# Gated linear attention feeding a softplus-erf expert layer on one core: most signs of the float64 weights written by ScalarE, and another fixed order of all steps

## The chip, the core and the metric

The kernel runs on one NeuronCore of a Trainium2 chip. The core has a matrix engine (TensorE, PE in the profile), a vector engine (VectorE, DVE), a scalar engine (ScalarE, ACT), GpSimd (POOL) and SyncE (SP), which here only issues DMAs. Matmuls accumulate in PSUM; the engines' other operands lie in SBUF. The metric is the device time of one execution, in microseconds (us). In this program a float32 product on PE appears as two records of the trace, and a product in the rounded format fp32r (`F32R`) as one.

## The reference, cut to what matters

```
def _attn_ref(q, k, v, alpha):                # each (4, 8, 768, 48)
    state = zeros((B, H, D, D)); y = zeros_like(q)
    for t in range(S):
        state = alpha[:, :, t, :, None] * state + einsum('bhd,bhe->bhde', k[:, :, t], v[:, :, t])
        y[:, :, t] = einsum('bhd,bhde->bhe', q[:, :, t], state)
    return y
def _moe_ref(x, w_in, w_out):                 # x (3072, 384), w_in (384, 2048), w_out (2048, 384)
    h = x @ w_in
    sp = np.maximum(h, 0.0) + np.log1p(np.exp(-np.abs(h)))
    return ((h * erf(sp)) @ w_out).astype(np.float32)
def reference(...):                           # x: the attention output, heads side by side
    x = attn_out.transpose(0, 2, 1, 3).reshape(B * S, H * D)
    return _moe_ref(x=x, **moe_kwargs)
```

`w_in` and `w_out` arrive as float64, everything else as float32.

## The kernel before, in words

**Order.** The whole program is a list of 1664 steps in the string `ORDER` (L31). The loop at its end runs through the list and calls the function of each step, and each of the four queues PE, DVE, ACT and SP executes its instructions exactly in that order: `Queue.call` (L211) chains every instruction to the one before it on its engine, which is why nearly all rows of the profile carry L211. Nothing is reordered at run time. An engine that waits holds up all its later instructions.

**Attention.** Time is cut into 12 parts of 64 steps, and the batch into two halves: 24 chunks n. Chunk n loads alpha, k, q, v (`la lk lq lv`); DVE runs two scans (`sb`, `sa`), takes a reciprocal (`rc`), scales k and q (`kk`, `qq`), masks the scores (`mk`) and updates the state (`td`, and `ta`, which is ACT's in the first two chunks). PE transposes k (`pn`) and makes the scores (`ps`), the outputs (`qt`, `sv`, into the single PSUM tile `py`) and the state's increment (`pu`); `pn`, `ps` and `pu` share one PSUM tile, `both`. ACT copies the transposed k (`kn`; `kd` does it on DVE), a small check value (`ic`), and rounds the result to `x_hi` (`xh`). The rest `x_lo` is made either by DVE as a difference (`xl`) or by PE, which adds minus·x_hi into `py` (`xp`, two products of 128x192), and by ACT, which copies it out (`xe`).

**Expert layer.** A block n of 256 tokens takes its x from chunks 2n and 2n+1. The 2048 hidden columns are 4 groups g of 512, each in two halves. `hm_n_g_half` is 18 products of 128x256 (hi·hi, lo·hi, hi·lo), into one of two PSUM buffers `h__111`, `h__112`; `he` (ACT) or `hd` (DVE) copies it out; `u n1 n2 n3 g` on ACT and `ma mb z1 z2` on DVE work out the activation on 128x1024, with ACT's tables changed between the two sets; `ga` (ACT) or `gd` (DVE) rounds the result to `gh`, `gl` (DVE) keeps the rest; `om_n_g_half` adds 12 products of 128x384 into `acc`. `oe` (ACT) or `ob` (DVE) scales the sums out, `od` stores them. All 24 chunks and 12 blocks are interleaved in `ORDER`.

**Weights.** They stay in SBUF as pairs hi, lo of fp32r. There are 12 tiles of `w_in` (128x512, steps `w?i_n`; group g uses tiles 3g to 3g+2) and 16 of `w_out` (128x384, `w?o_n`). A float64 number arrives as two 32-bit words, so a tile is 512 or 384 KB. The steps on one tile: `wl` loads it; `wy` (ACT) scales the high word into y; `wc` (ACT, from one byte) or `wv` (DVE, by a shift) makes the three low bits z; `wa` (DVE) makes z = (y << 3) | z, and `wb` (DVE, a second such pass) puts in the sign of y. `wh` (ACT) or `wk` (DVE) rounds z to hi; lo is made by DVE as a difference (`wq`), or by PE, z − hi into a PSUM buffer (`wp`, the same two buffers that `hm` uses), and a copy of ACT (`we`). Two more steps are in both files, unused before: `wd` (ACT) writes the high word, scaled, as a 16-bit float into the upper half of z, and so leaves its sign there; `wf` (ACT) writes the low bits as a 16-bit integer into the lower half. Together they stand in place of `wc` and `wb`.

**Dummy products.** `dw_n` issues n float32 products of the 128x128 identity, which nothing reads.

Of the kernel before, what the change touches and what calls it, by code (L numbers as in the profile page):

```python
# [36 lines left out]
wyo_2 xh_1 wbi_1 whi_1 wei_6 wpi_8 ta_0 la_2 sb_2 wao_2 wlo_12 wyo_12 dw_1 wpi_1 pn_1 wei_8 wbi_5 whi_5 wpi_5
wli_11 wco_12 kn_1 wbo_2 wei_1 wli_9 who_2 rc_2 ic_2 xl_1 wei_5 sa_2 hm_0_0_0 wao_12 td_2 lq_2 wyi_11 wbo_12
wlo_0 lk_2 wco_0 wqo_2 lv_2 wli_10 who_12 hm_0_0_1 kk_2 pu_1 qq_2 ps_2 wqo_12 wyo_0 wao_0 wci_9 wci_11 wai_11
he_0_0_0 la_3 sb_3 wbi_11 wbo_0 wci_10 wyi_10 he_0_0_1 wai_10 wyi_9 wai_9 lk_3 hm_0_1_0 mk_2 qt_2 u_0_0 rc_3  # L40
hm_0_2_0 sv_2 lq_3 ta_1 wbi_9 sa_3 wlo_1 wbi_10 he_0_1_0 whi_11 whi_9 who_0 td_3 wqi_11 la_4 qq_3 wvo_1 kk_3
wqo_0 he_0_2_0 whi_10 wyo_1 wao_1 sb_4 wqi_9 n1_0_0 xh_2 xl_2 pn_2 kn_2 n2_0_0 wqi_10 ic_3 hm_0_1_1 he_0_1_1
n3_0_0 hm_0_2_1 he_0_2_1 wbo_1 rc_4 who_1 pu_2 ps_3 wlo_3 wyo_3 lq_4 lk_4 wlo_7 mk_3 ta_2 qt_3 ma_0_0 g_0_0 sa_4
wlo_6 mb_0_0 wqo_1 hm_0_3_0 z1_0_0 wco_3 wao_3 lv_3 sv_3 xh_3 xl_3 kk_4 pn_3 he_0_3_0 wyo_7 hm_0_3_1 kn_3 ic_4
z2_0_0 td_4 lk_5 he_0_3_1 la_5 wco_7 wco_6 hm_1_0_0 qq_4 wlo_9 wyo_6 sb_5 u_0_1 wao_7 wbo_3 ga_0_0_0 gl_0_0_0
hm_1_1_0 he_1_0_0 ga_0_0_1 gl_0_0_1 wao_6 u_0_2 n1_0_1 pu_3 ps_4 n1_0_2 rc_5 n2_0_1 qt_4 om_0_0_0 hm_1_0_1 wbo_7
who_7 mk_4 ta_3 lv_4 sv_4 sa_5 td_5 who_3 wqo_3 kk_5 n3_0_1 he_1_1_0 ma_0_1 wbo_6 pn_4 wqo_7 mb_0_1 he_1_0_1
n2_0_2 kn_4 lq_5 qq_5 n3_0_2 who_6 ma_0_2 la_6 xh_4 xl_4 om_0_0_1 wyo_9 wco_9 wao_9 wqo_6 mb_0_2 g_0_1 z1_0_1
wlo_11 wyo_11 hm_1_2_0 he_1_2_0 wbo_9 lk_6 z2_0_1 lv_5 hm_1_3_0 he_1_3_0 g_0_2 z1_0_2 pu_4 wco_11 ps_5 mk_5 lq_6
wlo_8 wco_8 wyo_8 wlo_4 z2_0_2 qt_5 wao_8 ga_0_1_1 wlo_5 hm_1_3_1 he_1_3_1 hm_1_2_1 wco_4 wlo_13 wyo_4 wao_11  # L50
u_0_3 gl_0_1_1 hm_1_1_1 wlo_10 u_1_0 wbo_8 ta_4 ga_0_2_0 om_0_1_1 wbo_11 sv_5 ic_5 who_9 wqo_9 who_8 n1_0_3
gl_0_2_0 wqo_8 om_0_2_0 sb_6 he_1_1_1 lv_6 wao_4 td_6 ga_0_1_0 gl_0_1_0 pn_5 wbo_4 xh_5 he_1_2_1 rc_6 xl_5
hm_2_1_0 hm_2_1_1 wyo_5 who_11 wqo_11 wco_5 wko_4 sa_6 wao_5 qq_6 qt_6 kn_5 pu_5 wyo_10 wlo_14 wco_10 wbo_5
wao_10 kk_6 ps_6 n2_0_3 ga_0_2_1 n1_1_0 who_5 wqo_5 he_2_1_0 wqo_4 om_0_1_0 n3_0_3 gl_0_2_1 wbo_10 ma_0_3
he_2_1_1 wvo_13 hm_2_0_0 mb_0_3 n2_1_0 wyo_13 n3_1_0 wao_13 mk_6 ta_5 wbo_13 who_10 wqo_10 g_0_3 z1_0_3 he_2_0_0
hm_2_0_1 who_13 wqo_13 z2_0_3 wco_14 ma_1_0 pn_6 he_2_0_1 wyo_14 wlo_15 wco_15 wyo_15 wao_14 om_0_2_1 kn_6 sv_6
ga_0_3_0 gl_0_3_0 pu_6 wao_15 ga_0_3_1 gl_0_3_1 xh_6 wbo_14 lv_7 om_0_3_0 u_1_1 lk_7 wbo_15 g_1_0 mb_1_0
hm_2_2_0 ic_6 la_7 who_15 wqo_15 who_14 wqo_14 om_0_3_1 u_1_2 n1_1_2 oe_0_1 od_0_1 oe_0_0 hm_2_2_1 z1_1_0 z2_1_0
ga_1_0_0 sb_7 lq_7 rc_7 gl_1_0_0 gd_1_0_1 n1_1_1 lq_8 xl_6 sa_7 gl_1_0_1 om_1_0_0 n2_1_2 n2_1_1 om_1_0_1
he_2_2_0 qq_7 kk_7 hm_2_3_0 n3_1_1 td_7 ma_1_1 mb_1_1 n3_1_2 he_2_2_1 ps_7 mk_7 qt_7 hm_2_3_1 g_1_1 u_1_3 z1_1_1  # L60
z2_1_1 u_2_1 ic_7 ga_1_1_0 sv_7 xh_7 ta_6 la_8 ga_1_1_1 lv_8 ma_1_2 pn_7 gl_1_1_0 om_1_1_0 gl_1_1_1 om_1_1_1
# [885 lines left out]
```

## Time and profile before

| | |
|---|---|
| time, median of 3 runs | 516.24 us (515.7 to 516.78) |
| span of the profiled execution, first to last instruction | 513.9 us |
| PE busy | 504.0 us (98%) |
| DVE busy | 488.2 us (95%) |
| ACT busy | 465.8 us (91%) |
| POOL busy | 6.5 us (1%) |
| DMA moved | 43.69 MB, mean 85 GB/s |

The profiled execution's own time isn't listed apart from its span; the median of the runs is 2.3 us above that span. Shares are means over the whole span: the first 29 us, in which the first weights and the first two chunks are made ready, look unlike the rest, so the profile has to be read by stretches of time. Instructions on one engine overlap a little: the next one begins some 0.1 us before the former is shown to end, so what an instruction costs its engine is the distance from its start to the next one's start (its pitch) and not its own duration.

### The profile page before, as it was taken

What the parts mean: (1) busy time and instruction counts of PE and PEld (TensorE: products, weight loads), DVE (VectorE), ACT (ScalarE), POOL (GpSimd) and SP (SyncE); (2) the same over time, 40 slices, a digit from 0 to 9 for tenths busy, and PEclk for the clock granted to TensorE, in tenths of its full rate; (3) what the DMA queues carried; (4) which work ended last, traced back from release to release, by engine and by line L of the source; (5) the groups of instructions that cost most, each with busy time, mean ns of one, the idle gap of its engine ahead of it and who ended that gap; (6) DMA issues with size and microseconds to landing.
All of it is one profiled execution on the core that took longest, in us unless ns stands there. A gap on an engine that the chain in (4) does not pass through costs nothing.

```text
span 513.9 us, 16869 instructions
## 1 busy us (share of the span) xinstructions
PE 504.0 (98%) x7465; PEld 481.7 (94%) x7465; DVE 488.2 (95%) x655; ACT 465.8 (91%) x637; POOL 6.5 (1%) x41
## 2 busy tenths in 40 slices
...
GB/s 324 401 200 176 117 188 131 97 81 60 58 74 44 22 99 78 45 73 83 23 78 107 80 41 60 85 15 44 68 111 54 90 58 32 3 1 32 0 32 34
DMA packets 21387, 43.69 MB, mean 85 GB/s; under 512 B 2368, under 2 KB 5440, under 8 KB 21312
## 3 DMA queue, kind: packets, MB, share of 16 engines
...
q8 instruction: 59, 0.97, 0.8%
...
HBM read 37.86 MB, written 4.72 MB: 83 GB/s over the span
## 4 chain that ended last, share of the span: by engine, by line
PE 64%; DVE 18%; ACT 12%; issue 4%; DMA 1%; POOL 1%; DVEq 0%; POOLq 0%; ACTq 0%
PE acc L211 29%; PE h__112 L211 13%; PE h__111 L211 12%; PE both L211 4%; PE py L211 4%; DVE t L211 2%; DVE gl__104 L211 1%; ACT L211 1%; DVE gl__103 L211 1%; DVE w__98 L211 1%; DVE w__100 L211 1%; PE warm L211 1%; ACT w__97 L211 1%; DMA s__87<-in_moe_w_out_dram 1%; DVE w__97 L211 1%
## 5 line engine op out<-in xcount | busy, mean ns | idle before, releaser
L211 ACT ACT_TABLE_LOAD x64 | 82.1, 1283 | 1.9 <-PEq L901 0.9
L211 PE MATMUL acc<-wo_hi,gh__102 128*128 128x384 f32 x192 | 44.7, 346 | 0.1
L211 PE MATMUL acc<-wo_hi,gh__101 128*128 128x384 f32 x192 | 43.9, 348 | 0.1
L211 PE MATMUL acc<-wo_lo,gh__102 128*128 128x384 f32 x192 | 43.0, 337 | 0.2 <-DVE wo_lo L211 0.2
L211 PE MATMUL acc<-wo_hi,gl__104 128*128 128x384 f32 x192 | 43.1, 337 | 0.0
L211 PE MATMUL acc<-wo_lo,gh__101 128*128 128x384 f32 x192 | 41.6, 336 | 0.0
L211 PE MATMUL acc<-wo_hi,gl__103 128*128 128x384 f32 x192 | 41.6, 337 | 0.0
L211 PEld LDWEIGHTS acc<-wo_lo,gh__102 128*128 128x128 f32 x192 | 34.2, 188 | 0.5 <-DVE wo_lo L211 0.5
L211 PEld LDWEIGHTS acc<-wo_hi,gl__104 128*128 128x128 f32 x192 | 34.3, 188 | 0.0
L211 PEld LDWEIGHTS acc<-wo_hi,gl__103 128*128 128x128 f32 x192 | 34.0, 188 | 0.2 <-DVE gl__103 L211 0.2
L211 PEld LDWEIGHTS acc<-wo_lo,gh__101 128*128 128x128 f32 x192 | 34.1, 188 | 0.0
L211 PEld LDWEIGHTS acc<-wo_hi,gh__101 128*128 128x128 f32 x192 | 31.6, 188 | 1.9 <-DVE gh__101 L211 0.4
L211 PEld LDWEIGHTS acc<-wo_hi,gh__102 128*128 128x128 f32 x192 | 32.6, 188 | 0.8 <-DVE gh__102 L211 0.2
L211 DVE TENSOR_TENSOR_SCAN B<-raw_a,back 128x520 f32<-128x520 f32 x24 | 29.6, 1233 | 4.0 <-POOL T L266 3.9
L211 DVE TENSOR_TENSOR_SCAN A<-raw_a,start 128x520 f32<-128x520 f32 x24 | 29.6, 1233 | 0.2
L211 ACT ACTIVATE s__88<-s__88 128x1024 f32<-128x1024 f32 x22 | 23.2, 1056 | 1.0 <-DVE t L211 0.9
L211 ACT ACTIVATE s__86<-s__86 128x1024 f32<-128x1024 f32 x20 | 21.2, 1058 | 1.9 <-DVE t L211 1.8
L211 PE MATMUL h__112<-x_hi__107,wi_hi 128*128 128x256 f32 x144 | 21.7, 286 | 0.3 <-ACT wi_lo L211 0.3
L211 PE MATMUL h__111<-x_hi__107,wi_hi 128*128 128x256 f32 x144 | 21.4, 284 | 0.0
L211 PE MATMUL h__111<-x_hi__108,wi_hi 128*128 128x256 f32 x144 | 21.1, 282 | 0.0
L211 PE MATMUL h__112<-x_hi__108,wi_hi 128*128 128x256 f32 x144 | 21.1, 282 | 0.0
L211 PE MATMUL h__112<-x_lo__109,wi_hi 128*128 128x256 f32 x144 | 21.0, 281 | 0.0
...
## 6 DMA issues: line engine op xcount, KB each, us to landing
...
raw_k<-in_k_dram SPq DMA_DIRECT2D x24, 256.0 KB, 3.1
raw_q<-in_q_dram SPq DMA_DIRECT2D x24, 256.0 KB, 3.3
raw_v__113<-in_v_dram SPq DMA_DIRECT2D x12, 256.0 KB, 3.3
raw_v__114<-in_v_dram SPq DMA_DIRECT2D x12, 256.0 KB, 3.6
out_dram<-o__106 SPq DMA_DIRECT2D x12, 192.0 KB, 2.0
...
```

Source lines behind the costliest of these rows:

```text
L211: ins = made(*args, **kw)
```

## The change: another list of steps

No step's code is altered but one line of `hm`, which now asks whether the block's buffer exists instead of whether the half is 0, since the new list may begin with half 1. All else is the list, 1668 steps long. Counted in the two lists:

| steps | engine | before | after |
|---|---|---|---|
| `wb` sign as a second pass | DVE | 28 | 11 |
| `wc` low bits | ACT | 25 | 3 |
| `wv` low bits | DVE | 3 | 8 |
| `wd`, `wf` 16-bit halves | ACT | 0, 0 | 17, 17 (6 of `w_in`, 11 of `w_out`) |
| `wh` / `wk` rounding to hi | ACT / DVE | 27 / 1 | 11 / 17 |
| `xl` / `xp`+`xe` | DVE / PE+ACT | 24 / 0 | 19 / 5 (chunks 1, 2, 3, 4, 6) |
| `ga` / `gd` | ACT / DVE | 51 / 45 | 44 / 52 |
| `kn` / `kd` (22 that do work) | ACT / DVE | 20 / 2 | 17 / 5 |
| `oe` / `ob` | ACT / DVE | 18 / 6 | 12 / 12 |
| `dw` blocks (products) | PE | 4 (25) | 3 (24) |
| tiles with `wp` before `hm_0_0_0` | PE | 9 | 7 |
| runs of attention products between `hm` and `om` after `hm_0_0_0` | PE | 53 | 42 |

The core of the diff (the rest of the list differs in the same manner):

```
@@ ORDER, its beginning
-la_0 wli_2 wyi_2 wci_2 wli_3 wyi_3 wci_3 sb_0 rc_0 sa_0 wai_2 wbi_2 whi_2 wli_0 wyi_0 wci_0 wai_3 wbi_3 dw_14
+la_0 wli_2 wli_0 wyi_2 lk_0 sb_0 rc_0 sa_0 wci_2 wli_3 dw_14 ic_0 wyi_0 wfi_0 wai_2 wdi_0 kk_0 pn_0 wbi_2 wfi_3 lq_0
...
@@ ORDER, its end
-ma_11_3 ga_11_2_1 f3 mb_11_3 gl_11_2_1 g_11_3 z1_11_3 od_10_0 om_11_2_1 ga_11_2_0 gl_11_2_0 om_11_2_0 z2_11_3
-gd_11_3_1 gl_11_3_1 om_11_3_1 ga_11_3_0 gl_11_3_0 om_11_3_0 oe_11_0 od_11_0 oe_11_1 od_11_1
+od_10_1 ga_11_2_0 om_11_1_0 ma_11_3 g_11_3 od_10_0 gl_11_2_0 mb_11_3 ga_11_2_1 z1_11_3 gl_11_2_1 om_11_2_0 z2_11_3
+gd_11_3_1 om_11_2_1 gd_11_3_0 gl_11_3_1 gl_11_3_0 om_11_3_1 om_11_3_0 oe_11_1 f2 od_11_1 ob_11_0 f3 od_11_0
...
@@ hm
-            if half == 0:
+            if self.hs[g] is None:
                 self.hs[g] = self.pl.h.tile([P, GT * TB], F32, name="hs", tag="hs")
```

DVE's queue after its first two scans, before (`w__97` to `w__100` are the four buffers in which a weight tile is put together; a `SCALAR_TENSOR_TENSOR` with the name of a buffer on both sides is `wa` or `wb`, "x2" is both):

```order
L211 SCALAR_TENSOR_TENSOR w__97<-w__97 128x512 x2
L211 SCALAR_TENSOR_TENSOR w__98<-w__98 128x512 x2
L211 TENSOR_TENSOR raw_k_118<-raw_k_118,B 128x512
L211 SCALAR_TENSOR_TENSOR w__99<-w__99 128x512 x2
L211 TENSOR_TENSOR raw_q_116<-raw_q_116,A 128x512
L211 SCALAR_TENSOR_TENSOR w__100<-w__100 128x512
L211 SCALAR_TENSOR_TENSOR B<-raw_a,back 128x520
L211 TENSOR_TENSOR sT<-both,mask 128x512
L211 SCALAR_TENSOR_TENSOR w__100<-w__100 128x512
L211 SCALAR_TENSOR_TENSOR w__97<-w__97 128x512
L211 RECIPROCAL start<-B 128x8
```

The same place of DVE's queue after the change:

```order
L205 SCALAR_TENSOR_TENSOR w__97<-w__97 128x512
L205 TENSOR_TENSOR raw_k_118<-raw_k_118,B 128x512
L205 SCALAR_TENSOR_TENSOR w__97<-w__97 128x512
L205 SCALAR_TENSOR_TENSOR w__98<-w__98 128x512
L205 CAST wi_hi<-w__97 128x512
L205 CAST wi_hi<-w__98 128x512
L205 TENSOR_TENSOR raw_q_116<-raw_q_116,A 128x512
L205 TENSOR_SCALAR w__100<-hs__93 128x512
L205 SCALAR_TENSOR_TENSOR w__99<-w__99 128x512
L205 SCALAR_TENSOR_TENSOR B<-raw_a,back 128x520
L205 TENSOR_TENSOR sT<-both,mask 128x512
```

The pairs of passes have become single ones for tile 0 (`w__98`) and tile 3 (`w__99`), and the roundings to `wi_hi` (`CAST`, step `wk`) and one `wv` (`TENSOR_SCALAR`) have come in between.

PE's queue up to the first two thirds of `hm_0_0_0`, before (`h__…<-w__…,ident` and the row below it are one `wp`; `warm` is a dummy product, `both<-ident,raw_k` is `pn_1`):

```order
L211 MATMUL py<-sT,raw_v__114 32x64 x32
L211 MATMUL h__111<-w__99,ident 128x512
L211 MATMUL h__111<-wi_hi,minus 128x512
L211 MATMUL warm<-ident 128x128
L211 MATMUL h__112<-w__97,ident 128x512
L211 MATMUL h__112<-wi_hi,minus 128x512
L211 MATMUL both<-ident,raw_k_119 128x128 x4
L211 MATMUL h__111<-w__100,ident 128x512
L211 MATMUL h__111<-wi_hi,minus 128x512
L211 MATMUL h__112<-x_hi__107,wi_hi 128x256 x6
L211 MATMUL h__112<-x_hi__107,wi_lo 128x256 x6
```

The same place after the change:

```order
L205 MATMUL both<-ident,raw_k_119 128x128 x4
L205 MATMUL warm<-ident 128x128 x3
L205 MATMUL py<-sT,raw_v__114 32x64 x32
L205 MATMUL h__112<-w__99,ident 128x512
L205 MATMUL h__112<-wi_hi,minus 128x512
L205 MATMUL h__111<-w__98,ident 128x512
L205 MATMUL h__111<-wi_hi,minus 128x512
L205 MATMUL py<-x_hi__107,minus 128x192 x2
L205 MATMUL h__112<-x_hi__107,wi_hi 128x256 x6
L205 MATMUL h__112<-x_hi__107,wi_lo 128x256 x6
```

The block of one dummy product is gone, the two `wp` of tiles 8 and 5 no longer stand ahead of `hm_0_0_0`, and `xp_1` (`py<-x_hi__107,minus`) does.

ACT's queue, before, from the rounding of the second chunk's `x_hi` to the copy `wei_1` (its tenth row), which frees the PSUM buffer of `hm_0_0_0`:

```order
L211 ACTIVATE x_hi__107,sums<-py 128x2x3x64
L211 ACTIVATE wi_hi<-w__97 128x512
L211 ACTIVATE wi_lo<-h__112 128x512
L211 ACTIVATE T<-both 128x8x48
L211 ACTIVATE w__99<-s__86 128x384
L211 ACTIVATE wi_lo<-h__111 128x512
L211 ACTIVATE wi_hi<-w__100 128x512
L211 ACTIVATE w__99<-s__86 128x384
L211 ACTIVATE kn<-both 128x384
L211 ACTIVATE wi_lo<-h__112 128x512
L211 ACTIVATE wo_hi<-w__98 128x384
```

After the change, from the rounding of the second chunk's `x_hi` to the `wh` of tile 8:

```order
L205 ACTIVATE x_hi__107,sums<-py 128x2x3x64
L205 ACTIVATE wi_lo<-h__112 128x512
L205 ACTIVATE w__97<-hs__91 128x512
L205 ACTIVATE wi_lo<-h__111 128x512
L205 ACTIVATE x_lo__109<-py 128x2x3x64
L205 ACTIVATE w__97<-hs__91 128x512
L205 ACTIVATE inv<-start 128x8
L205 ACTIVATE wi_hi<-w__100 128x512
L205 ACTIVATE kn<-both 128x384
```

ACT's roundings `wi_hi` have left this place, `xe_1` (`x_lo__109<-py`) has come in, and the instructions on `w_out`'s tiles (128x384) come later.

## Rows read from the trace of the kernel before

**Rows 1.** First line of the profile's page.

```profile
span 513.9 us, 16869 instructions
```

**Rows 2.** Stretches from:to, then length, engines' busy time, granted clock, DMA share, GB/s.

```profile
10.00:29.00 19.00, 17.91 (x282) 11.06 (x281) 18.57 (x31) 18.57 (x41) 0.00 (x0) 1.00 1.03 400
29.00:514.00 485.00, 480.02 (x7154) 464.54 (x7154) 463.74 (x617) 441.21 (x588) 2.17 (x22) 1.00 0.22 68
```

**Rows 3.** Waits of PE's weight loads, 28 to 509 us: total, times, longest.

```profile
PEld h__112 L211 <- ACT wi_lo L211: 0.9, 1, 0.9
PEld acc L211 <- DVE wo_lo L211: 0.5, 1, 0.5
```

**Rows 4.** Timeline of PE, 0 to 34 us: start, duration, operation, idle before.

```profile
11.31 1.02 PE L211 MATMUL h__112<-w__98,ident 128*128 128x512 f32 x2
11.77 0.80 PE L211 MATMUL h__112<-wi_hi,minus 128*128 128x512 f32 x1
12.41 0.83 PE L211 MATMUL warm<-ident 128*128 128x128 f32 x6
...
28.88 0.99 PE L211 MATMUL h__112<-x_hi__107,wi_hi 128*128 128x256 f32 x6 [0.26 <-ACT wi_lo L211]
```

**Rows 5.** Timeline of ACT, 3 to 31 us.

```profile
5.04 1.22 ACT L211 ACTIVATE w__97<-hs__90 128x512 f32<-128x512 f32 x2 [2.56 <-DMA hs__90<-in_moe_w_in_dram]
...
13.33 1.23 ACT L211 ACTIVATE w__97<-hs__94 128x512 int32<-128x512 uint8 x2
14.45 1.25 ACT L211 ACTIVATE w__98<-hs__95 128x512 int32<-128x512 uint8 x2
...
27.36 0.59 ACT L211 ACTIVATE w__99<-s__86 128x384 int32<-128x384 uint8 x1
27.81 0.52 ACT L211 ACTIVATE kn<-both 128x384 f32<-128x384 f32 x1
28.18 0.64 ACT L211 ACTIVATE wi_lo<-h__112 128x512 fp32r<-128x512 f32 x1
```

**Rows 6.** Timeline of DVE, 3 to 31 us.

```profile
3.92 1.24 DVE L211 TENSOR_TENSOR_SCAN B<-raw_a,back 128x520 f32<-128x520 f32 x1 [3.92 <-POOL T L266]
...
20.68 0.55 DVE L211 TENSOR_TENSOR x_lo__109<-py,x_hi__107 128x384 fp32r<-128x384 f32 x1
21.15 0.68 DVE L211 SCALAR_TENSOR_TENSOR w__99<-w__99 128x512 int32<-128x512 int32 x1
21.75 0.68 DVE L211 SCALAR_TENSOR_TENSOR w__100<-w__100 128x512 int32<-128x512 int32 x1
...
23.55 0.35 DVE L211 TENSOR_SCALAR w__98<-s__85 128x384 int32<-128x384 int32 x1
```

**Rows 7.** DVE's groups by shape: busy, mean ns, idle before.

```profile
L211 DVE CAST gh__101<-hs__94 128x512 fp32r<-128x512 f32 x5 | 2.1, 423 | 0.1
```

**Rows 8.** Timeline of PE, 33 to 64 us.

```profile
35.14 0.88 PE L211 MATMUL h__112<-x_hi__107,wi_lo 128*128 128x256 f32 x6
35.85 0.86 PE L211 MATMUL h__112<-x_lo__109,wi_hi 128*128 128x256 f32 x6
36.65 0.86 PE L211 MATMUL py<-raw_q,T 48*32 48x64 f32 x64
37.43 0.97 PE L211 MATMUL h__111<-x_hi__107,wi_hi 128*128 128x256 f32 x6
38.25 0.87 PE L211 MATMUL h__111<-x_hi__107,wi_lo 128*128 128x256 f32 x6
```

**Rows 9.** DMA issues up to 30 us: KB each, median us to landing.

```profile
raw_v__114<-in_v_dram SPq DMA_DIRECT2D x1, 256.0 KB, 9.1
```

**Rows 10.** Records of the tile of dummy products in two stretches.

```profile
4.72:8.72 4.00, 4.00 (x19) 4.00 (x20) 1.00 1.03 396
8.72:9.94 1.22, 1.22 (x11) 1.03 (x9) 1.00 1.00 376
```

**Rows 11.** Timeline of SP's queue, 508 to 514 us.

```profile
510.40 0.33 SPq L211 DMA_DIRECT2D out_dram<-o__106  x1
```

More of the change, by code (lines that the diff above doesn't have):

```diff
@@ L37 @@
[L37 to L61, printed above, removed]
@@ L137 @@
[L137 to L139 removed]
+la_0 wli_2 wli_0 wyi_2 lk_0 sb_0 rc_0 sa_0 wci_2 wli_3 dw_14 ic_0 wyi_0 wfi_0 wai_2 wdi_0 kk_0 pn_0 wbi_2 wfi_3 lq_0
+wai_0 wki_2 wdi_3 wli_7 wyi_3 kn_0 wki_0 wyi_7 qq_0 wpi_2 la_1 wli_6 wvi_7 wai_3 lv_0 sb_1 wei_2 wli_1 wpi_0 whi_3
@@ new lines @@
+wei_0 ps_0 wpi_3 mk_0 wyi_6 rc_1 wai_7 pu_0 lk_1 wfi_6 lq_1 wei_3 sa_1 wli_4 wdi_6 kk_1 wbi_7 qq_1 wki_7 ic_1 wai_6
+wfi_1 wdi_1 wvi_4 lk_2 dw_7 sv_0 ps_1 xh_0 wyi_4 wyi_1 mk_1 wli_8 lv_1 wai_1 whi_6 wpi_7 ta_0 wli_10 wei_7 wpi_6 pn_1
+dw_3 wyi_8 wfi_8 wai_4 wei_6 xl_0 wbi_4 sv_1 wki_1 wfi_10 la_2 wdi_8 wki_4 wlo_2 wpi_4 lq_2 wpi_1 xh_1 sb_2 wai_8
+wei_4 xp_1 wdi_10 wli_5 wei_1 rc_2 wli_11 xe_1 wyi_10 td_2 ic_2 sa_2 kk_2 hm_0_0_0 whi_8 wai_10 kn_1 hm_0_0_1 wyi_11
+wvi_11 wyo_2 wqi_8 wlo_6 pu_1 la_3 he_0_0_0 wvi_5 qq_2 ps_2 wlo_0 wyi_5 sb_3 wli_9 he_0_0_1 whi_10 wfo_2 wdo_2 ta_1
@@ new lines @@
+hm_1_1_1 om_0_0_1 wlo_8 g_0_2 rc_6 sv_5 z1_0_1 z1_0_2 z2_0_1 wlo_11 wfo_8 wyo_8 pn_5 wfo_9 lk_6 wyo_9 wdo_8 lq_7 wlo_4
+wdo_9 wao_8 lq_6 z2_0_2 gd_0_1_1 kk_6 he_1_2_1 xh_5 wlo_5 who_7 kn_5 wqo_7 wlo_13 gl_0_1_1 wao_9 wfo_11 hm_1_3_1
+gd_0_2_0 wdo_11 wyo_11 wfo_4 xl_5 sa_6 he_1_1_1 wlo_14 ic_6 he_1_3_1 td_6 om_0_1_1 wao_11 gl_0_2_0 wdo_4 ga_0_2_1
+wko_11 gl_0_2_1 wyo_4 la_7 qq_6 lk_7 u_0_3 who_8 who_9 hm_2_1_0 hm_2_1_1 pu_5 n1_0_3 sb_7 he_2_1_1 ps_6 wqo_8 wyo_5
+wqo_9 qt_6 mk_6 wco_5 wao_4 n2_0_3 om_0_2_0 wqo_11 wao_5 ta_5 wbo_5 kk_7 who_4 rc_7 lv_7 n3_0_3 wko_5 wvo_14 sa_7 sv_6
@@ new lines @@
+he_4_1_1 om_3_1_0 n2_4_0 ma_3_2 lq_12 mk_11 mb_3_2 lq_14 la_12 ta_10 n3_4_0 gd_3_1_1 gl_3_0_0 om_3_0_0 n3_3_3 sv_11
+sb_12 ga_3_0_1 lv_12 pn_11 ma_3_3 u_4_2 gl_3_0_1 hm_4_3_0 kd_11 gl_3_1_1 td_12 hm_4_3_1 om_3_1_1 xh_11 rc_12 xl_11
+g_3_2 od_2_1 g_3_3 sa_12 lk_13 mb_3_3 ma_4_0 he_4_3_1 ic_12 om_3_0_1 z1_3_2 he_4_3_0 z1_3_3 z2_3_2 hm_5_1_0 lk_12
+qq_12 n1_4_2 kk_12 la_13 u_4_1 n1_4_1 qt_12 gd_3_2_1 sb_13 g_4_0 mb_4_0 u_4_3 gl_3_2_1 ps_12 ga_3_2_0 z2_3_3 pu_11
+he_5_1_0 mk_12 gl_3_2_0 rc_13 hm_5_1_1 om_3_2_1 n2_4_2 hm_5_0_0 ga_3_3_1 n2_4_1 sa_13 om_3_2_0 ta_11 n3_4_2 z1_4_0
@@ new lines @@
+pn_12 kk_13 lv_13 sv_12 lq_13 gl_3_3_1 td_13 ic_13 qq_13 ma_4_2 kn_12 xh_12 hd_5_1_1 ga_3_3_0 n1_4_3 ps_13 la_14 pu_12
+n3_4_1 gl_3_3_0 om_3_3_1 hm_5_2_0 mb_4_2 he_5_2_0 z2_4_0 he_5_0_0 g_4_2 ma_4_1 sb_14 om_3_3_0 g_4_1 rc_14 xl_12
+hm_5_2_1 ob_3_1 u_5_1 mk_13 mb_4_1 hm_5_0_1 ga_4_0_0 he_5_2_1 sv_13 u_5_2 lv_14 n2_4_3 ta_12 gd_4_0_1 n3_4_3 sa_14
+n1_5_2 pn_13 ob_3_0 ic_14 z1_4_2 td_14 gl_4_0_1 z2_4_2 hd_5_0_1 qt_13 gl_4_0_0 hm_5_3_0 om_4_0_0 n1_5_1 ma_4_3 z1_4_1
+n2_5_1 om_4_0_1 gd_4_2_1 u_5_0 he_5_3_0 lk_14 lk_15 g_4_3 xh_13 kn_13 z2_4_1 gl_4_2_1 od_3_0 gd_4_2_0 n2_5_2 la_15
@@ new lines @@
+gl_4_2_0 kk_14 om_4_2_1 om_4_2_0 sb_15 gd_4_1_0 xl_13 n1_5_0 hm_6_1_0 n2_5_0 rc_15 ic_15 qq_14 qt_14 gl_4_1_0 ps_14
+pu_13 mb_4_3 ga_4_1_1 sa_15 ta_13 hm_5_3_1 n3_5_2 td_15 z1_4_3 om_4_1_0 gl_4_1_1 n3_5_1 he_6_1_0 n3_5_0 ma_5_1
+om_4_1_1 z2_4_3 mk_14 hm_6_2_0 sv_14 la_16 hd_5_3_1 mb_5_1 lv_15 gd_4_3_1 g_5_1 pn_14 xh_14 lq_15 hm_6_1_1 gd_4_3_0
+he_6_2_0 u_5_3 kk_15 gl_4_3_1 ma_5_0 gl_4_3_0 om_4_3_1 z1_5_1 hm_6_2_1 mb_5_0 z2_5_1 sb_16 qq_15 kn_14 od_3_1 g_5_0
+he_6_1_1 he_6_2_1 gd_5_1_1 lq_16 xl_14 u_6_1 n1_5_3 om_4_3_0 gd_5_1_0 hm_6_0_0 rc_16 qt_15 z1_5_0 he_6_0_0 ps_15 pu_14
@@ new lines @@
+z2_5_0 gl_5_1_1 hm_6_0_1 ma_5_2 ob_4_0 n1_6_1 od_4_0 mk_15 n2_6_1 sv_15 ta_14 lq_17 n2_5_3 lk_16 oe_4_1 lv_16 pn_15
+mb_5_2 om_5_1_1 n3_5_3 n3_6_1 ma_5_3 g_5_2 td_16 gl_5_1_0 xh_15 lk_17 sa_16 mb_5_3 ga_5_0_1 z1_5_2 om_5_1_0 hm_6_3_0
+ga_5_0_0 la_17 gl_5_0_1 ma_6_1 gl_5_0_0 om_5_0_1 ic_16 u_6_2 he_6_3_0 he_6_0_1 mb_6_1 om_5_0_0 hm_6_3_1 qq_16 g_5_3
+xl_15 z2_5_2 kk_16 qt_16 ga_5_2_1 g_6_1 sb_17 kn_15 u_6_0 od_4_1 ps_16 pu_15 ga_5_2_0 gl_5_2_1 he_6_3_1 hm_7_0_0
+z1_6_1 ta_15 u_6_3 mk_16 om_5_2_1 gl_5_2_0 rc_17 ic_17 kk_17 z1_5_3 om_5_2_0 z2_6_1 sa_17 pn_16 qq_17 kd_16 sv_16
```

148 lines of the change are left out of this document (68 added, 80 removed).

## The prediction

> **What bounds the kernel now.** I read the page first: the span is 513.9 us [rows 1]. Then the table by stretches, since the page's shares mix two stages [rows 2]. From 29 us to the end PE is busy for 480 of 485 us, at a granted clock of 1.00; DVE has 21 and ACT 44 us to spare there. From 10 to 29 us it is the other way round: DVE and ACT are busy for 18.6 of 19 us each, and PE, which shows 17.9 us, has weight loads for 11.1 only, against 464.5 of 485 later. DMA runs at 1.03 of its share, 400 GB/s, in the same stretch, and so is full too. Third, the waits of PE after 28 us: the largest is 0.9 us, the next 0.5 [rows 3]. So there are two stages: a start, in which DVE and ACT make the first weights and the first x, until `hm_0_0_0` begins at 28.88 after a wait for ACT's copy of `wi_lo` [rows 4], and then 481 us in which PE goes from product to product. The time is the start of `hm_0_0_0`, plus PE's work behind it, plus what PE waits for, plus the tail. The change touches all four.
>
> **The start.** Before, `hm_0_0_0` stood behind nine `wp` and behind ACT's `wei_1` at 28.18 [rows 5]. By the lists, ACT issues 48 steps from its start at 5.04 to there, and 39 after; DVE 38 and 36; PE does two `wp` and one block of dummies less. Which engine is then late? DVE, up to the `wk` of tile 4, whose `wp` is next to last ahead of `hm_0_0_0`:
> - 4 scans at 1.15 us (1.24 less an overlap of 0.08): 4.6; 2 reciprocals at 0.12, an estimate: 0.2
> - 10 passes `wa`/`wb` at 0.60 (21.15 to 21.75): 6.0; 6 of attention of the same size: 3.6; one `xl` at 0.47 (20.68 to 21.15) [rows 6]
> - 5 casts `wk` at 0.34 (0.42 less the overlap) [rows 7]: 1.7; 2 `wv` of 512 columns at 0.34 (the 384 form takes 0.35 [rows 6], less the overlap, times 4/3): 0.7
>
> That is 17.3 us from 3.92 [rows 6], with about 0.85 of waits (an estimate: PE's scores and the first loads) 22.1. Then on PE two `wp` at 1.10 each (11.31 to 12.41 [rows 4]) and `xp_1` 0.25 (below): 24.6. ACT's steps up to its last copy for `hm_0_0_0` come to 18.6 us at 0.56 for a 512-column step (13.33 to 14.45), 0.45 for 384 and 0.37 for `kn` [rows 5], from 5.04 with 1.7 of idle time (estimate): 25.3. I take 25.2: **3.7 us earlier**, between 2.5 (a us more of waits) and 4.3. The 16-bit writes `wd` and `wf` show in no row. The lower bound is a plain 32-bit copy, `kn` at 0.37 for 384 columns, 0.5 for 512; the byte read of `wc` into 32 bits takes 0.45 and 0.56 [rows 5]; the upper bound is twice that, if each half-filled word is written like a whole one of its own. I take 0.56 and 0.45, of the nearest row, which reads every eighth byte.
>
> **PE's work behind it.** Two `wp` now come later: 2 x 1.10 = +2.2. Four more `xp`: 2 products of 128x192 each. A product of 256 columns costs 0.71/6 = 0.118 (35.14 to 35.85 [rows 8]), so 192 columns cost 0.089 and an `xp` 0.18; at the price of the dummies, 0.11 per record of 128 columns and two records a product [rows 10], it would be 0.67. I take 0.25, near the first, since its operands are fp32r as those of `hm` are: +1.0. The isolated gap in the Trainium skill, "TensorE: Matmul & The Clock Gate", section "Back-to-back issue gap", makes 192 columns 82 ns, an `xp` 0.165 and the sum 0.3 us less than mine; the 0.118 of the row for 256 columns is above that formula's 0.109. Then the runs of attention products: `hm` parts stand 0.71 apart, but 0.80 from the last part to a run behind it (35.85 to 36.65) and 0.82 within the first part after one (37.43 to 38.25) [rows 8], so a run costs 0.2 at its edges: 11 fewer, −2.2. Where `ps` now stands beside other products than `pu`, I allow −0.2 (estimate). Sum **+0.8**, from 0 to +2.5.
>
> **Waits.** The `wb` passes removed (17, 6 at 0.60 and 11 at 0.47: 8.8 us of DVE) are paid with 16 `wk` (about 5), 5 `wv` (1.7), 3 `kd`, 7 `gd`, 6 `ob`: DVE ends 2 to 4 us fuller, and ACT 7 us emptier, of 464 and 441 busy in 485 us [rows 2]. Neither becomes the bound over the whole. But in the stretch where weights and expert layer overlap both are as full as before, and 3.7 us less time lies ahead of it. Loads are the other side: DMA was already full to 29 us, the longest load took 9.1 us from issue to landing [rows 9], and what PE wants is wanted 3.7 us sooner. Adding up each engine's instructions in the new order, each started when its engine and what it waits for are done, gives PE's end 2.0 to 3.0 us earlier for DMA at 360 to 400 GB/s. I take **+0.5** for waits that before did not have, −0.3 to +3.
>
> **The tail.** The last store of before is issued at 510.40 [rows 11]. The new list issues `od_11_1` behind the last product and `od_11_0` behind it, one issue later: +0.35 to +0.45, and if the two stores slow each other, up to +0.9. I take **+0.5**. `f2`, `f3` and the read of the flag are covered by the store's landing.
>
> **Sum:** −3.7 +0.8 +0.5 +0.5 = −1.9: a span of 512.0 us, and as the median lies 2.3 above the span, 514.3; I state 514.2, rounded toward the addition by engines, whose middle is a little lower.
>
> **Rivals.**
> - *Waits give the gain back.* The loads of the weights bind: `hm_0_0_0` starts 3.7 us sooner, but `w_out` and the late tiles land when they did. For it: DMA at 1.03 until 29 us. Against: it falls to a mean of 0.22 after, and the two largest waits of PE are for ACT and DVE [rows 2, 3]. It takes back 1.5 to 2: 515.7 to 516.2.
> - *The 16-bit halves cost twice* (the other side). 12 of 34 lie on `w_in` (0.56 more each) and 22 on `w_out` (0.45): 6.7 + 9.9 = 16.6 us of ACT in its full stretch. The 12 stand ahead of `hm_0_0_0` in ACT's queue, which is the last to be ready there: 25.2 + 6.7 = 31.9, 3 later than before. That alone makes 514.2 + 6.7 = 520.9; with all of the 9.9 it is 530.8. Some of those ACT catches up on; by the addition PE ends 8 to 9 later than before: 524.5. The point from which it decides is 0.2 us more per step: twelve of those use up the forecast's gain. Against it: a read of single bytes spread over 384 columns takes 0.45, a plain copy 0.37 [rows 5], so an odd access costs a fifth and not double.
> - *PE's clock.* Three blocks of dummies instead of four lie ahead of `hm_0_0_0`. In before, 19 records of dummies take 4.00 us and later 11 take 1.22 [rows 10]: 0.21 and 0.11 each, so PE does pass from one of its two levels (1.2 and 2.4 GHz) to the other there, although the granted clock of the rows reads 1.00 in both. The Trainium skill, "TensorE: Matmul & The Clock Gate", section "What's actually happening", says that the default is throttled and that activity releases it, which speaks against taking activity out. If it falls back once for a stretch with two `hm` (each 2.13 long, twice that at half the clock) that is +4.3 at most, in part covered by waits: about 516.3. Against: `wp`, scores and outputs keep PE as dense as before, and 24 of 25 dummies stay.
> - *A larger gain.* No waits at all and the cheap end of PE's work: −3.7 −0 +0.35: 512.9.
>
> **How the numbers follow.** The likeliest case has 0.55 and its own range 512.7 to 515.6. The larger gain 0.10, waits 0.19, the 16-bit writes 0.08, the clock 0.05, and 0.03 for something that I have not seen. 0.2%, 1.0 us, is about what a measurement of this kernel can tell from no change. Faster by more (under 515.2): most of the first two, 0.50 + 0.10, and a little of the waits: 0.62. Same (515.2 to 517.3): 0.05 + 0.14 + 0.04: 0.24 with a hundredth of the unknown. Slower: 0.14. The range, 511.5 to 517.7, takes in the cheap bounds below and the waits' and clock's rivals above; the 16-bit rival lies outside.
>
> **What would show it right or wrong.** In the profile after: `hm_0_0_0` at about 25.2, waited for by its `xp_1` or ACT's copy. A step `wd` or `wf` at 0.65 for 512 columns; at 1.2 the second rival holds. `xp` at 0.2 to 0.3. PE's end 2 to 3 us earlier, with no wait above 1 us between; a wait of `om_0_…` on `wo_lo` or of a `wp` on a load would be the first rival. Two stores issued back to back at the end, the second one about 0.4 us behind. Dummies of 0.21 us or `hm` parts of 1.4 instead of 0.71 beyond 10 us would be the third. The prediction is wrong if the start gains less than 2 us or if PE's work behind it grows by over 2.5.

## The result and the profile after

The changed kernel takes 521.13 us (median of 4 runs, 520.02 to 521.72) against 516.02 for the kernel before in the same comparison: a ratio of 1.0088, interval 1.0064 to 1.0112. By the medians it is 5.1 us slower, by the ratio 4.5 (3.3 to 5.8); 514.2, faster, was forecast.

The profiled execution took 521.49 us, its span 519.8, so 1.7 lie outside the span. The engines' busy time, first lines of the page (span; busy us, share, instructions):

```profile
span 519.8 us, 16894 instructions
...
PE 505.3 (97%) x7473; PEld 484.3 (93%) x7473; DVE 485.5 (93%) x671; ACT 456.8 (88%) x621; POOL 6.8 (1%) x41
```

ACT has 9 us of work less than before and DVE 3 less, PE 1.3 more, and the span is 5.9 us longer. The stretches that stood in [rows 2] (from:to, length, PE, PE loads, DVE, ACT, POOL, clock, DMA share, GB/s):

```profile
10.00:29.00 19.00, 18.00 (x299) 12.71 (x298) 18.21 (x33) 18.23 (x38) 0.00 (x0) 1.00 0.96 368
29.00:520.00 491.00, 481.25 (x7148) 465.50 (x7146) 462.68 (x634) 433.57 (x576) 2.45 (x22) 1.00 0.23 69
```

Behind 29 us PE is now idle for nearly 10 of 491 us, where it was 5 of 485, but most of that is the tail behind the last product: up to the last product it is 2.7 of 483.9 us against 0.8 of 480.9. The clock is 1.00 throughout. PE's timeline around the first hidden product (answers to [rows 4]: start, duration, operation):

```profile
25.12 1.02 PE L205 MATMUL h__111<-w__98,ident 128*128 128x512 f32 x2
25.58 0.79 PE L205 MATMUL h__111<-wi_hi,minus 128*128 128x512 f32 x1
26.21 0.36 PE L205 MATMUL py<-x_hi__107,minus 128*128 128x192 f32 x2
26.41 0.89 PE L205 MATMUL h__112<-x_hi__107,wi_hi 128*128 128x256 f32 x6
```

`hm_0_0_0` begins at 26.41 and not at 28.88, behind `xp_1`, which costs 0.20. The last product ends at 512.85 and not at 509.84. So the profiled executions compare like this, each row from the start of `hm_0_0_0`, the end of the last product and the span:

| us | before | after | moved | forecast |
|---|---|---|---|---|
| start of `hm_0_0_0` | 28.88 | 26.41 | −2.5 | −3.7 |
| from there to the end of the last product | 481.0 | 486.4 | +5.5 | +1.3 |
| from there to the end of the span | 4.1 | 6.9 | +2.8 | +0.5 |

**The start.** ACT's timeline shows what the 2.5 instead of 3.7 is made of (in brackets: idle time before, and what ended it):

```profile
7.95 1.96 ACT L205 ACTIVATE w__98<-hs__91 128x512 f32<-128x512 f32 x3 [1.51 <-DMA hs__91<-in_moe_w_in_dram]
...
23.43 0.79 ACT L205 ACTIVATE w__100<-hs__90 128x512 f16<-128x512 f32 x1
24.07 0.48 ACT L205 ACTIVATE x_hi__107<-py 128x384 fp32r<-128x384 f32 x1
```

The third load, here tile 0, landed 1.5 us after ACT wanted it. In the old list the third load is another tile (tile 3), of the same size and also issued at 1.81. In a later profile of the old order (the experiment before_flag_late), ACT waited 2.0 for its third load, and `hm_0_0_0` began at 30.14:

```profile
8.43 1.22 ACT L206 ACTIVATE w__98<-hs__91 128x512 f32<-128x512 f32 x2 [1.99 <-DMA hs__91<-in_moe_w_in_dram]
```

So the profile of before had a lucky load. Over the profiles with the old start (28.88, 30.14, 29.11, 29.10) and with the new one (26.41, 26.71, 25.73, 26.94) the means are 29.3 and 26.4: the start is 2.9 us earlier. Where the third load let ACT begin at the same time, at 7.1 (before_stores_swapped and stores_swapped) or at 8.3 to 8.4 (before_flag_late and tail_both), it is 3.4 and 3.2 earlier. In the mean of four that load came 0.6 us later in the new order; whether by chance or by the other loads beside it isn't shown. DVE, which the forecast took to be the late engine, waited 1.45 us for the load of the first k, where 0.85 was allowed for all its waits:

```profile
8.60 0.69 DVE L205 TENSOR_TENSOR raw_k<-raw_k,B 128x512 f32<-128x512 f32 x1 [1.45 <-DMA raw_k<-in_k_dram]
```

A 16-bit step takes 0.64 us for 512 columns (23.43 to 24.07), a seventh more than the 0.56 that was taken.

**PE behind it.** Summed by kind from one step's start to the next one's, the 5.5 us are: two `wp` 2.25 and four `xp` 0.9; waits, 3.9 against 1.9, if a step from one product to the next counts as a wait where it is over 0.15 us longer than the median of its kind; the attention products and the edges around them, which were to be 2.4 shorter, about 0.3 longer. The waits of PE's loads behind 24 us, against 0.9 and 0.5 in [rows 3] (total, times, longest):

```profile
PEld acc L205 <- DVE gl__104 L205: 0.8, 1, 0.8
...
PEld h__112 L205 <- ACT hs__96 L205: 0.6, 1, 0.6
PEld h__111 L205 <- DVE wi_hi L205: 0.6, 1, 0.6
PEld acc L205 <- ACT gh__101 L205: 0.6, 1, 0.6
```

No single wait is large; they add up. One belongs to the new work itself: at 36 us the second product of `wp_5` waits for DVE's rounding (`DVE wi_hi`), 0.3 of the 2.25 us. What stands behind the others is read below, in the part on the prediction.

**The tail.** SP's queue at the end, for [rows 11], and the landing of the two stores (KB, us from issue to landing):

```profile
513.40 0.33 SPq L205 DMA_DIRECT2D out_dram<-o__106  x1
513.82 0.38 SPq L205 DMA_DIRECT2D out_dram<-o__105  x1
```

```profile
out_dram<-o__106 SPq DMA_DIRECT2D x1, 192.0 KB, 1.9
out_dram<-o__105 SPq DMA_DIRECT2D x1, 192.0 KB, 4.3
```

The second store is issued 0.4 us behind the first, as forecast, and then takes 4.3 us, where a store took 1.9 before.

### The profile page after: what moved, and what is told of

Its sections match the earlier page's. It is cut to its first block, busy times and chain, and to the rows that moved or that the text cites. A ratio compares the mean times of both kernels' runs of the same rounds, so it can differ in the third digit from the quotient of the medians.

```text
span 519.8 us, 16894 instructions
## 1 busy us (share of the span) xinstructions
PE 505.3 (97%) x7473; PEld 484.3 (93%) x7473; DVE 485.5 (93%) x671; ACT 456.8 (88%) x621; POOL 6.8 (1%) x41
## 4 chain that ended last, share of the span: by engine, by line
PE 65%; DVE 16%; ACT 13%; issue 3%; DMA 2%; SPq 0%; ACTq 0%; DVEq 0%
PE acc L205 30%; PE h__112 L205 13%; PE h__111 L205 13%; PE py L205 4%; PE both L205 4%; ACT L205 2%; ACT w__100 L205 1%; ACT s__88 L205 1%; DVE B L205 1%; DVE w__98 L205 1%; DMA hs__91<-in_moe_w_in_dram 1%; ACT w__97 L205 1%; ACT w__98 L205 1%; DVE w__100 L205 1%; ACT w__99 L205 1%
## 5 line engine op out<-in xcount | busy, mean ns | idle before, releaser
L205 PE MATMUL acc<-wo_hi,gl__104 128*128 128x384 f32 x192 | 43.2, 338 | 0.5 <-DVE gl__104 L205 0.5
L205 PE MATMUL acc<-wo_hi,gh__101 128*128 128x384 f32 x192 | 42.6, 341 | 0.6 <-ACT gh__101 L205 0.4
L205 PE MATMUL acc<-wo_hi,gh__102 128*128 128x384 f32 x192 | 43.0, 338 | 0.0
L205 PE MATMUL acc<-wo_hi,gl__103 128*128 128x384 f32 x192 | 41.5, 337 | 0.0
L205 PEld LDWEIGHTS acc<-wo_hi,gl__104 128*128 128x128 f32 x192 | 34.2, 188 | 0.8 <-DVE gl__104 L205 0.8
L205 PEld LDWEIGHTS acc<-wo_hi,gl__103 128*128 128x128 f32 x192 | 34.2, 188 | 0.0
L205 PEld LDWEIGHTS acc<-wo_hi,gh__102 128*128 128x128 f32 x192 | 33.4, 188 | 0.1
L205 PEld LDWEIGHTS acc<-wo_hi,gh__101 128*128 128x128 f32 x192 | 32.2, 188 | 1.3 <-ACT gh__101 L205 0.6
L205 ACT ACTIVATE s__88<-s__88 128x1024 f32<-128x1024 f32 x22 | 23.3, 1058 | 3.6 <-DVE t L205 3.4
L205 ACT ACTIVATE s__86<-s__86 128x1024 f32<-128x1024 f32 x18 | 19.1, 1059 | 7.6 <-DVE t L205 7.5
L205 PE MATMUL h__111<-x_hi__107,wi_hi 128*128 128x256 f32 x156 | 23.7, 287 | 0.0
L205 PE MATMUL h__112<-x_hi__108,wi_hi 128*128 128x256 f32 x156 | 23.5, 286 | 0.0
L205 PE MATMUL h__111<-x_hi__107,wi_lo 128*128 128x256 f32 x156 | 22.7, 281 | 0.0
L205 PE MATMUL h__112<-x_hi__108,wi_lo 128*128 128x256 f32 x156 | 22.7, 281 | 0.0
L205 PE MATMUL h__112<-x_lo__110,wi_hi 128*128 128x256 f32 x156 | 22.6, 281 | 0.0
```

What stands on the lines that cost most here:

```text
L205: ins = made(*args, **kw)
```

## Experiments

My first theory for the tail was the flag: `f2` and `f3` stand at the very end of the new list, so that the branch on the flag loads instructions while the last stores run (16 KB in one packet of 0.9 us at 515.85, by the trace's DMA packets; with the flag early, in flag_early, it lies at 511.80). The rival was the stores' own order. For the rest: the signs by ACT, the `xp`, the late `wp`, and the price of a run of attention products, each undone or done alone.

### flag_early

```
-... gl_11_1_0 om_11_1_0 ... ma_11_3 ... mb_11_3 ... oe_11_1 f2 od_11_1 ob_11_0 f3 od_11_0
+... gl_11_1_0 f2 om_11_1_0 ... ma_11_3 ... f3 mb_11_3 ... oe_11_1 od_11_1 ob_11_0 od_11_0
```

> The new order with the two flag steps f2 and f3 put back to where the old list has them (f2 ahead of om_11_1_0, f3 ahead of mb_11_3); nothing else moves. Late-flag theory: the end of the program reads the flag and branches, and with f2 and f3 behind the last product the loads of instructions (queues 8 and 14) fall beside the last stores; early again, the second store lands in about 2 us instead of 4.3, and the time falls by 2.0 to 2.5 us, from 521.1 to about 518.8. Store-order theory (two stores issued 0.4 us apart slow each other): no change, within 0.4 us.

519.95 us, ratio to before 1.0065 (1.0051 to 1.0079): 1.2 us less than the 521.13 of the changed kernel, half of what the theory wanted, and by the intervals alone not clear of the changed kernel. In its profile the second store takes 2.7 us, and 5.3 lie behind the last product.

### stores_swapped

```
-om_11_3_0 oe_11_1 f2 od_11_1 ob_11_0 f3 od_11_0
+om_11_3_0 ob_11_0 od_11_0 oe_11_1 f2 od_11_1 f3
```

> The new order with the last two stores exchanged on SyncE: od_11_0 as soon as its half is scaled, about 0.9 us ahead of od_11_1; f2 and f3 stay late. Store-order theory: the last store has the DMA engines to itself, and the time falls by 2 to 2.5 us, to about 518.8. Late-flag theory: only the one issue goes, 0.4 us less, and the last store still lands late: 520.7.

518.89 us, ratio 1.0053 (1.0041 to 1.0065): 2.2 us less, with the flag left late. Each store lands as fast as one alone (KB, us to landing), and 4.2 us lie behind the last product:

```profile
out_dram<-o__105 SPq DMA_DIRECT2D x1, 192.0 KB, 1.8
out_dram<-o__106 SPq DMA_DIRECT2D x1, 192.0 KB, 1.8
```

### before_flag_late

```
-... f2 om_11_1_0 ... f3 mb_11_3 ... oe_11_0 od_11_0 oe_11_1 od_11_1
+... om_11_1_0 ... mb_11_3 ... oe_11_0 od_11_0 oe_11_1 f2 od_11_1 f3
```

> The old order with f2 and f3 moved to the end as the new list has them; nothing else moves. Late-flag theory: 2.0 to 2.5 us slower than before, about 518.2. Store-order theory: no change, 516.0, at most 0.2 us from the flag itself.

515.99 us, ratio 0.9998 (0.9989 to 1.0007). A late flag costs nothing where the stores stand a microsecond apart; its 16 KB packet starts there at 513.05, just as the last store's packets have ended. The flag theory, as the cause by itself, falls.

### before_stores_swapped and tail_both

```
-oe_11_0 od_11_0 oe_11_1 od_11_1
+oe_11_0 oe_11_1 od_11_1 od_11_0
```

> The old order with its last two stores in the new list's order (od_11_1 behind the last product, od_11_0 one issue later); the flag steps stay early. Store-order theory: the second of two stores issued 0.4 us apart lands 0.8 us or more later than a store alone, and with the later issue the time rises by 1.2 us, to about 517.3. Issue-only theory (the prediction's): +0.4, 516.5.

> The new order with both tails put back: stores exchanged and f2, f3 early. If the store order is all that counts, the time equals stores_swapped, 518.9; if the late flag costs by itself, it is 1 us less, 517.9. In neither case is it below the old order's 516.1, since PE's work behind hm_0_0_0 is 5 us longer and begins only 3 us earlier.

The old order with the stores exchanged takes 517.53 us, ratio 1.0024 (1.0015 to 1.0033): +1.2, and its second store lands late by the same 0.8 as in flag_early:

```profile
out_dram<-o__106 SPq DMA_DIRECT2D x1, 192.0 KB, 2.1
out_dram<-o__105 SPq DMA_DIRECT2D x1, 192.0 KB, 2.7
```

tail_both takes 518.82 (ratio 1.0048, 1.0034 to 1.0061), the same as stores_swapped. So: two stores 0.4 us apart cost 1.2 us; with the late flag's instruction loads beside them another 1.2, which the landing times show (4.3 against 2.7) better than the medians; the late flag without them nothing. All of it goes with the order of two stores. It is 2.2 of the 5.1 us.

### sign_back

```
 # the 17 tiles t with wf_t:   -wf_t ... wd_t ... wa_t     +wc_t ... wa_t wb_t
```

> The new order, but for the 17 tiles whose sign ScalarE makes: wf is replaced by wc in its place, wd is left out, and wb stands right behind wa. ScalarE has 17 instructions less and VectorE 17 more. If the two 16-bit steps are what loses (ScalarE is the later engine in the first 100 us), the time falls by 2 us or more. If the signs are worth what they were meant to be (VectorE is the later one, five second passes of 0.60 us lie ahead of the first hidden product), it rises by 2 to 3 us, to 523 to 524. If waits just move from one engine to the other, it stays within 1 us.

528.59 us, ratio 1.0237 (1.0222 to 1.0252): 7.5 us slower than the changed kernel, well over the 2 to 3 expected. From 29 to 110 us DVE is busy for 80.2 of 81 us there and ACT for 68.4 (columns as above, sign_back first); in the changed kernel they share the load, 78.8 and 79.2:

```profile
29.00:110.00 81.00, 76.65 (x1535) 70.40 (x1534) 80.24 (x136) 68.44 (x118) 0.59 (x6) 1.00 0.47 152
```

```profile
29.00:110.00 81.00, 80.06 (x1571) 74.67 (x1570) 78.83 (x135) 79.22 (x134) 0.72 (x6) 1.00 0.48 155
```

With the rest of this order held, the signs by ACT save 7.5 us: the loss isn't theirs.

### before_sign

```
 # 14 of those tiles, in the old list:   -wc_t ... wa_t wb_t     +wf_t wd_t ... wa_t
```

> The old order with nothing changed but the sign of 14 tiles (those of the new order's 17 that use wc): wf in the place of wc, wd right behind it, wb left out. VectorE loses 14 passes (7.5 us), ScalarE gains 14 instructions at 0.56 to 0.65 (8.4 us), 5 of them ahead of hm_0_0_0. The old order's chain ran on ScalarE up to 64 us, so if that engine is the late one, hm_0_0_0 begins 3 us later and the time rises by 3 to 6 us, to 519 to 522. If the signs are a gain by themselves, as sign_back may suggest (7.5 us more without them), the time falls by 1 us or more.

524.07 us, ratio 1.0157 (1.0143 to 1.0171): 8 us slower than before, more than the 3 to 6 expected. `hm_0_0_0` begins at 32.62, behind ACT's copy:

```profile
32.62 0.97 PE L206 MATMUL h__112<-x_hi__107,wi_hi 128*128 128x256 f32 x6 [0.76 <-ACT wi_lo L206]
```

From 29 to 110 us ACT is busy for 80.8 of 81 us and DVE for 71.7:

```profile
29.00:110.00 81.00, 77.87 (x1451) 72.62 (x1454) 71.71 (x111) 80.80 (x142) 0.49 (x5) 0.98 0.41 138
```

The clock's mean of 0.98 there is one stretch at the lower level, in this execution. Two others, with a granted clock of 1.000 throughout, took 523.5 and 524.1, so the loss doesn't hang on it.

### xl_back and wq_59

```
 # from stores_swapped; xl_back:   -xp_n ... xe_n   +... xl_n      (n = 1, 2, 3, 4, 6)
 # wq_59:                          -wpi_n ... wei_n +... wqi_n     (n = 5, 9)
```

> The new order with the last two stores exchanged (stores_swapped, 518.9 us), and in the five chunks 1, 2, 3, 4, 6 the rest x_lo made by VectorE again: xp left out, xl in the place of xe. If the xp are plain work of PE that VectorE could have taken, PE's work behind hm_0_0_0 falls by 0.9 us and the time to about 518. If VectorE is the late engine of the first 100 us, its five passes of 0.47 us come back as waits of PE and the time rises to 519.5 to 521.

> stores_swapped (518.9 us), and the rest of the weight tiles 5 and 9 of w_in made by VectorE (wq in the place of we) and not by PE (wp) and ScalarE. PE has two wp of 1.13 us less behind hm_0_0_0. If that work is what the new order lost, 2.2 us come back: 516.7. If VectorE is the late engine there, its two passes of 0.6 us return as waits: between 517.5 and 519.

xl_back takes 523.54 us (1.0126, 1.0105 to 1.0148) and wq_59 526.0 (1.0177, 1.0151 to 1.0204): 4.7 and 7.1 us more than stores_swapped, though PE has 0.9 and 2.3 us of work less, and more than I expected. The executions differ widely (521.4 to 524.4 and 523.0 to 529.6), and the profiles are of the slowest of each. VectorE is late in both, but it isn't all of the loss. In xl_back the two largest waits are these:

```profile
35.60 1.15 PE L206 MATMUL h__112<-x_hi__107,wi_lo 128*128 128x256 f32 x5 [2.02 <-issue]
106.73 0.85 PE L206 MATMUL py<-raw_q,T 48*32 48x64 f32 x64 [2.28 <-issue]
```

The second ends as DVE's `xl` frees `py`, at 106.63. The first lies in the middle of a group of hidden products and ends with no semaphore of any engine; it is taken up again with the waits below. In wq_59 PE waits for `wi_lo` of DVE (total, times, longest):

```profile
PEld h__111 L206 <- DVE wi_lo L206: 4.6, 1, 4.6
```

and then pays a second time, in the clock (eighth number behind the length: from 36 us on 1.00, 0.57, 0.58, 1.00):

```profile
36.00:40.00 4.00, 2.67 (x79) 2.20 (x77) 4.00 (x9) 3.97 (x6) 0.00 (x0) 1.00 0.46 135
40.00:44.00 4.00, 0.93 (x4) 0.94 (x5) 4.00 (x9) 0.19 (x2) 0.00 (x0) 0.57 0.53 183
44.00:48.00 4.00, 4.00 (x23) 4.00 (x22) 2.04 (x3) 2.40 (x4) 0.00 (x0) 0.58 0.00 0
48.00:52.00 4.00, 4.00 (x147) 3.69 (x147) 3.37 (x7) 3.87 (x9) 0.10 (x1) 1.00 0.02 4
```

PE had 0.93 us of products in the four from 40 to 44, and the granted clock was at its lower level, 1.2 GHz, for much of that stretch and the next. The same happens once more at 65 us, behind a wait of 2.3 us in mid-group: from 66 to 70 us the granted clock is 0.50.

### pn_behind_sv

```
 # the old list:   -sv_8 ... om_2_1_0 pn_8     +sv_8 pn_8 ... om_2_1_0     (chunks 5, 8, 9, 12, 13, 19)
```

> The old order with the transposes pn of the chunks 5, 8, 9, 12, 13, 19 moved from a place of their own among hidden and output products to right behind an sv or qt; the copies kn follow where they would come too early. Six runs of attention products less. By the price of the prediction, 0.2 us a run, PE's work falls by 1.2 us. By what the new order's trace shows (a pn takes 0.41 us behind an sv and 0.355 behind a full-array product, and what stands behind it pays 0.09 in either place), it falls by 0.04 each, 0.25 in all, and the time stays at 516.0 to 516.2 but for new waits.

518.6 us, ratio 1.0047 (1.0031 to 1.0063). In four of these chunks (8, 9, 13, 19) the transposes now overwrite, in `both`, the increment of the chunk before ahead of its `ta`, so that the state that comes out is another; the instructions are the same. PE's work did not fall by anything like 1.2: hidden and output products, `pn` and `sv` take 439.3 us from start to start without the waits, against 439.5 before, too close to tell 0.25 from nothing. The 2.5 us are new waits (total, times, longest):

```profile
PEld both L206 <- DVE raw_q L206: 1.2, 1, 1.2
PEld both L206 <- DVE sT L206: 1.0, 1, 1.0
```

## Why the prediction was wrong

**The start** held in kind: `hm_0_0_0` is 2.9 us earlier in the mean of the profiles, 3.7 was taken and 2.5 to 4.3 allowed. DVE's 17.3 us and `xp`'s 0.25 were near: 17.7 and, alone between other products, 0.20 were measured. The Trainium skill, "TensorE: Matmul & The Clock Gate", section "Back-to-back issue gap", made an `xp` 0.165, less than the trace shows. What is missing went into the waits of DVE and ACT for the first loads, 1.45 and 1.51 us. What the sum did not say: this gain is a loan. Two `wp` and four `xp` come back behind it, 3.1 us, and they were counted, but as if cheaper things paid for them. Counting the plain durations of the hidden, output and attention products that PE has done, the new order is some 2.5 us ahead of the old one at 30 us into the profile and 0.6 behind at 50.

**The failed step is "11 fewer, −2.2" with the −0.2 behind it.** Of the 6.9 us between forecast and result it is the largest part, 2.7; the waits are 1.5, the tail 1.7, the start 0.8. With it the prediction's own sign of being wrong came, PE's work behind the start growing by over 2.5: it grew by 3.4. I took the price of a run from an output product's neighbours, `qt` [rows 8], and multiplied it by the runs that vanish. But those that vanish are mostly transposes that stood alone, 16 of 20 before, and such a run was nearly free. The kernel before, PE (start, duration, operation):

```profile
151.54 0.87 PE L211 MATMUL acc<-wo_lo,gh__102 128*128 128x384 f32 x4
152.25 0.87 PE L211 MATMUL acc<-wo_hi,gl__104 128*128 128x384 f32 x4
152.96 0.60 PE L211 MATMUL both<-ident,raw_k 128*128 128x128 f32 x4
153.31 0.94 PE L211 MATMUL acc<-wo_hi,gh__101 128*128 128x384 f32 x4
154.09 0.86 PE L211 MATMUL acc<-wo_lo,gh__101 128*128 128x384 f32 x4
```

0.71 from the last part to the transpose, as between any two parts; 0.35 for itself; 0.78 for the part behind it, 0.08 too much. After, where it stands behind `sv`:

```profile
277.64 0.86 PE L205 MATMUL py<-sT,raw_v__114 64*32 64x64 f32 x64
278.43 0.66 PE L205 MATMUL both<-ident,raw_k 128*128 128x128 f32 x4
278.84 0.94 PE L205 MATMUL acc<-wo_hi,gh__101 128*128 128x384 f32 x4
279.62 0.85 PE L205 MATMUL acc<-wo_lo,gh__101 128*128 128x384 f32 x4
```

0.79 for `sv`, 0.41 for the transpose, 0.78 for the part behind it. Joining the two saves one edge of 0.1 and makes the transpose 0.06 dearer. Nor did the swap of `ps` and `pu` give anything: 0.59 + 0.40 in the old order, 0.515 + 0.47 in the new one. And the count of 42 had left out three runs that hold only an `xp`; with them 45 remain, and of the 53 one held only the flag's product. −2.4 was forecast, +0.3 came.

**The waits** were +2.0 and not +0.5. They are seven of 0.4 to 0.8 us, from 33 to 509 us. In the four profiles of the new list whose start and middle are the same (the changed kernel, flag_early, stores_swapped, tail_both) the waits come to 3.8 to 5.4 us, in three of the old list (before, before_flag_late, before_stores_swapped) to 1.6 to 2.0. The traces show where four of the seven come from.

Three are late loads, one step removed, which is the first rival's mechanism. DVE waits for an alpha at 200 us, runs from there to its `qq_12` without a gap, and `qt_12` waits 0.8 us for that:

```profile
200.20 1.24 DVE L205 TENSOR_TENSOR_SCAN B<-raw_a,back 128x520 f32<-128x520 f32 x1 [1.14 <-DMA raw_a<-in_alpha_dram]
...
212.08 0.69 DVE L205 TENSOR_TENSOR raw_q<-raw_q,A 128x512 f32<-128x512 f32 x1
212.87 0.85 PE L205 MATMUL py<-raw_q,T 48*32 48x64 f32 x64 [0.74 <-PE h__112 L205]
```

In flag_early, stores_swapped and tail_both DVE waits 1.62, 0.53 and 1.40 there and `qt_12` 1.28, 0.20 and 1.07: each time the wait for the load, less 0.33. The buffer of that alpha was free at 183.4, but its load is issued at 195.9: in SP's queue it stands behind a store whose half ACT has scaled only at 193.6. In the same way ACT waits half a microsecond each for two tiles of `w_out`, at 76.8 and 83.4, and runs without a gap to the copies that PE waits for at 80.2 and 94.9. None of the three profiles of the old list has a wait of DVE or ACT for a load behind 30 us.

The first of the seven is of another kind, a stop within a group of products:

```profile
32.55 0.85 PE L205 MATMUL h__112<-x_hi__107,wi_hi 128*128 128x256 f32 x5
33.83 0.39 PE L205 MATMUL h__112<-x_hi__107,wi_hi 128*128 128x256 f32 x1 [0.43 <-issue]
```

It lies behind the same count of PE's products, 474 records of the trace, in every profile that has it: 0.6 us here, 0.2 in flag_early, 1.3 in tail_both, 0.7 in wq_59 and 2.2 in xl_back, where the same count falls two products further on in the list. PE goes on 1.4 to 1.6 us after the end of a 16 KB packet of instructions each time (here 32.28 and 33.83). So PE seems to have come to the end of the instructions that it had; the profiles of the old list reach that count at 37 us or later, over 3 us after that packet, and don't stop; stores_swapped, where the packet ended 1.1 us earlier, doesn't either. No run tests this. It also means that part of xl_back's and wq_59's loss isn't VectorE's.

**The tail** was "+0.35 to +0.45, and if the two stores slow each other, up to +0.9", and it came as 2.2 in the runs and 2.8 in the profile. The sentence that `f2`, `f3` and the read of the flag are covered by the store's landing was wrong too, though only together with the stores' order.

**The rivals.** The first came nearest, and in part by its own mechanism. The 16-bit writes are a seventh dearer than taken, not twice: 12 times 0.08 on `w_in` and 22 times some 0.05 on `w_out` is 2 us of ACT. The argument that an odd access costs a fifth was a wrong reading: `kn`'s 0.37 is a copy out of PSUM, and a plain copy of 384 columns from the same source as the byte read takes 0.45 too. The time did rise, but sign_back shows that it is not on the signs' account. The clock stayed at 1.00 from 9.3 us on through all products of the changed kernel with one block of dummies less. In wq_59 it fell where PE stood still, which agrees with the Trainium skill, "TensorE: Matmul & The Clock Gate", section "What's actually happening", that activity releases the throttle.

**The account.** 5.1 us: −2.9 for the start, +3.1 for the work put behind it, +0.3 for the edges, +2.0 for waits, +2.2 for the tail, together 4.7. What stays open is how much of the waits an earlier load, or an earlier packet of instructions, would take back: none was tried by itself, and three waits, at 131, 394 and 508 us, end with ACT's or DVE's work on the activations and were not followed further. No experiment here points to a version below both kernels: the best of the new order is stores_swapped, 2.7 us above the old one.
